# Carrying the first attention states on TensorE in a linear-attention and MLP kernel

## The chip, the cores and the metric

The kernel runs on one core of a Trainium2 chip. A core has five engines, each with its own instruction queue that it works off in order: TensorE (PE, matrix products into PSUM; its weight loads are listed apart as PEld), VectorE (DVE), ScalarE (ACT), GpSimd (POOL) and SyncE (SP), which here only issues DMAs. Engines wait for each other through semaphores. The metric is the device time of one execution in microseconds (us).

## The reference

The first half is a causal linear attention with a decay `lam` per head; its output, four batches of 768 tokens by 8 heads of 64, is read as 3072 tokens by 512 and goes through an MLP with a leaky ReLU. All is float32 in value; the two MLP weights come as float64.

```python
for b in range(nb):                      # blocks of 64 tokens
    intra = np.einsum('bhic,bhjc->bhij', qb, kb) * Dmask[None]
    intra = np.einsum('bhij,bhjd->bhid', intra, vb)
    inter = np.einsum('bhid,bhde->bhie', qb * lam_pow[None], kv_state)
    out[:, :, sl] = intra + inter
    kb_dec = kb * rev_pow[None]
    kv_state = lam_block[None, :, None, None] * kv_state + np.einsum('bhsd,bhse->bhde', kb_dec, vb)
...
h = x @ w_in                             # 3072 x 512 by 512 x 2048
g = np.maximum(0.01 * h, h)
return (g @ w_out).astype(np.float32)    # 2048 x 512
```

## The kernel before

**Attention.** The tokens are worked in 24 chunks of 128, that is two blocks of 64 per chunk, six chunks per batch. For a chunk `c`, `load_kq` and `load_v` bring keys, queries and values (two buffers each, by `c % 2`); `transposes` turns keys and queries on PE (L425), copies them from PSUM on ACT (L436, L437), scales the keys by the decay (L441, written for DVE or GpSimd) and the queries by its powers (L445: on DVE for the first QS chunks, on GpSimd after). `scores` makes on PE, in quarter-array products (helper `quad`, L335), the scores (`go`) and the two state products of the chunk (`kv`, into `pu[0]` and `pu[1]`); both lie in the PSUM tile psc, the scores in the lower and the state products in the upper half of each of its two banks. DVE multiplies the scores by the decay mask (L474) and adds the state products into one of four state tiles (L479 for the first of a batch, L481 for the others); GpSimd scales each state by the decay of a block into the next state tile (L484). `outputs` makes the chunk's result on PE: `own` (scores by values), then `inter` (state by queries) in two halves with a small copy between them (L513). The result is split at once into three parts for products in a reduced format: xh on ACT (L529), xl and xm on DVE (L530, L532).

**MLP.** Four chunks are a token group (512 tokens, six groups). The columns of the first weight are taken in eight panels `p` of 256. `w_in` loads a panel as float64 in two halves (L589, three raw buffers), turns it to float32 (ACT L610, L612, L614; DVE L616, L617) and splits it into three parts (L623 or L625, L628, L643). A unit `up(g, p)` multiplies group `g` with panel `p`: for each of two blocks of 128 columns twelve PE products (L723) into one of three PSUM banks, a rescaling on ACT (L742) between its second and third part, and the leaky ReLU on ACT (L747). Results are stored to DRAM (L754, or sums of them, L791) and read back for the second product, which runs in units of its own (`strassen`, `plain`, `ending`; L851 on PE, with loads by L825 and splits by L828, L831, L835), in parts by a Strassen scheme. Finished banks are transposed on DVE (L943) and stored (L951).

**What sets the order.** Nothing is issued directly: `add` records each step with an engine (or a choice of two), an estimated duration and the keys of the buffers that it reads and writes. `Plan.emit` orders all of them by a list scheduler: it starts each step at the earliest time that the estimates allow, and where several could start, the one of the lower rank. The rank is the position in the list `seq`, corrected by a step's own rank. `seq` is written out by hand for its first part: `('a', c)` is a whole chunk, `('b', 4)` loads and prepares chunks 4 and 5 and makes the scores of 4, `('r', c)` is a round that finishes chunk `c`, prepares `c + 2` and makes the scores of `c + 1`, `('wi', p)` prepares a panel, `('up', g, p, ...)` is a unit. Later units follow `ORDER`. The prices LEAD0 and LEAD advance the loads of the second product's units in rank, WSR delays the sums of the second weight (`w_sums`), and TURN_B sets where the rotation over the three PSUM banks starts. Where the plan expects PE to be idle for over 0.4 us, it inserts transposes of an identity matrix into an unused bank (`busy`, L282); nine more stand at the start.

## Time and profile before

| | us |
|---|---|
| median of three timed runs | 599.52 |
| lowest, highest | 599.29, 600.74 |
| the profiled execution | 598.83 |
| its span, first to last instruction | 597.1 |
| PE busy in the span | 586.2 |
| DVE, ACT, POOL busy in the span | 406.7, 299.2, 134.0 |

The granted TensorE clock is at full speed in all slices of the span. A busy share over the whole span is a mean over stages with different limits: in the first 60 us attention and the first units are worked together, from then on PE products follow each other almost without a gap, and the last 4.5 us are the drain of the output. In the lists, L and a number is a line of the kernel before; "a <- b" after a line is what was waited for; an entry with x and a number stands for that many instructions.

### The profile page before, as it was taken

What the parts mean: (1) busy time and instruction counts of PE and PEld (TensorE: products, weight loads), DVE (VectorE), ACT (ScalarE), POOL (GpSimd) and SP (SyncE); (2) the same over time, 40 slices, a digit from 0 to 9 for tenths busy, and PEclk for the clock granted to TensorE, in tenths of its full rate; (3) what the DMA queues carried; (4) which work ended last, traced back from release to release, by engine and by line L of the source; (5) the groups of instructions that cost most, each with busy time, mean ns of one, the idle gap of its engine ahead of it and who ended that gap; (6) DMA issues with size and microseconds to landing.
All of it is one profiled execution on the core that took longest, in us unless ns stands there. A gap on an engine that the chain in (4) does not pass through costs nothing.

```text
span 597.1 us, 13281 instructions
## 1 busy us (share of the span) xinstructions
PE 586.2 (98%) x5336; PEld 485.0 (81%) x5336; DVE 406.7 (68%) x559; ACT 299.2 (50%) x468; POOL 134.0 (22%) x170
## 2 busy tenths in 40 slices
PE   7899999999999999999999999999999999999997
PEld 6778888888888888888788888888888888888886
DVE  4999883357365565465389889965689695788652
ACT  3788884345555565565598874331344223252300
POOL 2654770835636348121000000000000000000000
PEclk9999999999999999999999999999999999999999
DMA  8999855975899999886788865526467547394533
GB/s 205 238 292 242 245 171 132 247 195 132 240 284 260 239 269 232 247 259 224 244 273 273 298 196 206 162 89 190 128 198 223 175 144 193 121 259 164 177 107 70
DMA packets 163949, 123.04 MB, mean 206 GB/s; under 512 B 100400, under 2 KB 140592, under 8 KB 163888
## 3 DMA queue, kind: packets, MB, share of 16 engines
q1 hardware_dynamic: 148128, 112.75, 64.4%
q10 hardware_dynamic: 13200, 5.77, 3.8%
q0 software_dynamic: 2560, 3.68, 2.5%
q8 instruction: 42, 0.69, 0.5%
q14 instruction: 19, 0.16, 0.1%
HBM read 81.27 MB, written 40.89 MB: 205 GB/s over the span
## 4 chain that ended last, share of the span: by engine, by line
PE 91%; DVE 5%; DMA 2%; ACT 0%; issue 0%; SPq 0%; DVEq 0%
PE b L723 43%; PE po L851 13%; PE b L851 12%; PE psc L851 11%; PE pt L851 4%; PE po L335 4%; PE psc L335 3%; DMA xm<-g 1%; DVE wl L628 1%; DVE w L617 1%; DMA attb<-in_q_dram 1%; DVE w L616 1%; PE pt L425 1%; DVE att L474 0%; DVE xl L530 0%
## 5 line engine op out<-in xcount | busy, mean ns | idle before, releaser
L723 PE MATMUL b<-xh,wh 128*128 128x512 f32 (+2 forms) x392 | 103.6, 387 | 0.8 <-ACT xh L529 0.8
L723 PE MATMUL b<-xm,wm 128*128 128x512 f32 (+2 forms) x392 | 103.7, 393 | 0.0
L723 PE MATMUL b<-xl,wl 128*128 128x512 f32 (+2 forms) x392 | 103.5, 386 | 0.1
L828 ACT ACTIVATE xh<-xm 128x1024 fp32r<-128x1024 f32 x46 | 48.8, 1060 | 86.6 <-DMA xm<-g 40.9
L723 PEld LDWEIGHTS b<-xh,wh 128*128 128x128 f32 x392 | 72.7, 188 | 16.1 <-ACT xh L529 0.9
L723 PEld LDWEIGHTS b<-xl,wl 128*128 128x128 f32 x392 | 72.8, 188 | 15.2 <-DVE wl L628 0.5
L723 PEld LDWEIGHTS b<-xm,wm 128*128 128x128 f32 x392 | 71.2, 188 | 15.1 <-ACT b L742 0.4
L742 ACT ACTIVATE b<-b 128x512 f32<-128x512 f32 (+2 forms) x97 | 56.1, 581 | 54.5 <-PE b L723 54.4
L747 ACT ACTIVATE gs<-b 128x512 f32<-128x512 f32 (+2 forms) x97 | 56.8, 591 | 39.7 <-PE b L723 34.6
L831 DVE SCALAR_TENSOR_TENSOR xl<-xm,xh 128x1024 fp32r<-128x1024 f32 x46 | 56.0, 1218 | 26.4 <-ACT xh L828 25.5
L835 DVE SCALAR_TENSOR_TENSOR xm<-xl,xh 128x1024 fp32r<-128x1024 f32 x50 | 61.2, 1224 | 3.5
L484 POOL TENSOR_TENSOR att<-att 128x256 f32<-128x256 f32 x40 | 34.9, 873 | 37.9 <-DVE att L481 37.9
L616 DVE TENSOR_SCALAR w<-w 128x512 int32<-128x512 int32 x32 | 22.6, 706 | 27.2 <-ACT w L610 27.1
L396 POOL DMA_DIRECT2D attb<-in_q_dram x64 | 39.5, 624 | 2.9 <-issue 1.4
L445 POOL TENSOR_TENSOR att<-att 128x512 f32<-128x512 f32 (+1 forms) x20 | 24.9, 1244 | 63.4 <-PE po L335 47.4
L441 POOL TENSOR_TENSOR attb<-attb,att 128x512 f32<-128x512 f32 (+1 forms) x23 | 26.1, 1136 | 34.6 <-PE po L425 10.5
L851 PE MATMUL psc<-xm,wm 128*128 128x512 f32 x84 | 32.8, 391 | 0.1
L851 PE MATMUL psc<-xh,wh 128*128 128x512 f32 x84 | 32.7, 389 | 0.0
L851 PE MATMUL psc<-xl,wl 128*128 128x512 f32 x84 | 32.7, 389 | 0.0
L474 DVE TENSOR_TENSOR att<-psc,att 128x512 f32<-128x512 f32 x24 | 16.5, 688 | 21.9 <-PE psc L335 21.8
L617 DVE CUSTOM_DVE_ANT_0 w<-w,lows 128x1024 uint16<-128x1024 uint16 x32 | 26.2, 818 | 7.1 <-ACT lows L614 6.2
L828 ACT ACTIVATE raws<-raws 128x1024 fp32r<-128x1024 f32 x12 | 12.7, 1061 | 27.6 <-DMA raws<-g 18.1
(184 smaller groups left out, 1096.3 us busy)
## 6 DMA issues: line engine op xcount, KB each, us to landing
xm<-b SPq DMA_DIRECT2D x28, 512.0 KB, 3.8
g<-gs SPq DMA_DIRECT2D x27, 512.0 KB, 4.6
xm<-g SPq DMA_DIRECT2D x22, 512.0 KB, 4.2
b<-gs SPq DMA_DIRECT2D x20, 512.0 KB, 3.9
raws<-in_moe_w_in_dram SPq DMA_DIRECT2D x16, 512.0 KB, 5.2
raws<-in_moe_w_out_dram SPq DMA_DIRECT2D x16, 512.0 KB, 4.9
attb<-in_k_dram SPq DMA_DIRECT2D x48, 128.0 KB, 4.7
attb<-in_v_dram SPq DMA_DIRECT2D x24, 256.0 KB, 4.7
```

The source lines that it names most:

```text
L335: nc.tensor.matmul(dst[HALF[cols]], lhsT=lhsT[HALF[rows]], rhs=rhs[HALF[rows]], start=start, stop=True, skip_group_check=True)
L396: (move if nm == "k" else carry)(0.55 if nm == "k" else QSL, lambda o=o, z=z, e=nc.sync if nm == "k" else nc.gpsimd: e.dma_start(out=o.rea ...
L484: add("POOL", 0.7, lambda new=new, j=j: nc.gpsimd.tensor_tensor(state[(j + 1) % 4], new, _bc(lam_c, 2, D), op=ALU.mult), [f"st{j % 4}", "f ...
L616: add("DVE", 0.42, lambda: nc.vector.tensor_scalar(d, d, 3, None, op0=ALU.logical_shift_left), [], [key])
L617: add("DVE", 1.0, lambda: nc.vector.tensor_tensor(d, d, low, op=ALU.add), [kl], [key])
L723: nc.tensor.matmul(dst, lhsT=w[z][:, kk * 2 * P + f * P:kk * 2 * P + (f + 1) * P], rhs=x[z][:, kk, toks], start=start and kk == 0, stop=kk ...
L742: add("ACT", ns, lambda b=b: nc.scalar.activation(out=b, in_=b, func=AF.Copy, bias=0.0, scale=S + 1.0), [], [kb], rank=-1.5)
L747: add("ACT", t, lambda o=o, x=s_: nc.scalar.activation(out=o, in_=x, func=AF.Prelu, bias=0.0, scale=(1.0 + 1.0 / S) / (WS * U), alpha=0.01 ...
L828: nc.scalar.activation(out=ring[j][0], in_=g(), func=AF.Copy, bias=0.0, scale=NEAR)
L831: nc.vector.scalar_tensor_tensor(ring[j][1], g(), 1.0, ring[j][0].bitcast(F32), op0=ALU.mult, op1=ALU.subtract)
L835: nc.vector.scalar_tensor_tensor(m, l.bitcast(F32), -S, h.bitcast(F32), op0=ALU.mult, op1=ALU.add)
L851: nc.tensor.matmul(dst, lhsT=lhs(z), rhs=ring[j][z][:, col:col + n], start=first and z == 0, stop=z == 2, skip_group_check=True)
```

## The change

The scores and the two state products get keys of their own in the plan (psc, pu0, pu1, and "began", which keeps PE's order in the shared banks). For the first two chunks (PEC = 2) the state is no longer scaled by GpSimd and added by DVE: PE multiplies the previous state by a diagonal matrix `carry_on`, which holds the block decay of each head and is built once on DVE (`factors_c`), and adds it to the state product in PSUM; ACT copies the sum to the state tile. From the last state of chunk 1 on, GpSimd and DVE carry it as before. QS goes from 4 to 2, so that the queries of chunks 2 and 3 are scaled by GpSimd; KM goes from 2 to 4, so that the keys of chunks 2 and 3 may be scaled by DVE or GpSimd, as the plan finds. TURN_B, WSR and LEAD0 are set anew. The first part of `seq`, `ORDER` and the order of some units of the first Strassen part are new. The plan gets an entry without an instruction that takes 0.45 us of the DMA queue's planned time for each output store that ACT issues.

```diff
-    QS = 4
-    KM = 2
+    QS = 2
+    KM = 4
+    PEC = 2
-    TURN_B = 2
-    HOLD, WPR, WSR, LEAD0 = 0.15, 2.0, 0.0, 12.0
+    TURN_B = 1
+    HOLD, WPR, WSR, LEAD0 = 0.15, 2.0, 2.0, 8.0
...
+    def factors_c():
+        nc.vector.tensor_tensor(carry_on, _bc(ident, 1, HP), _bc(lam_c, 2, P), op=ALU.mult)
...
+    carry_on = gst[:, 1, 0, :].rearrange("p (y t) -> p y t", y=HP)
+    add("DVE", 0.7, factors_c, ["fq"], ["gs1"])
...
         if c < GOFIRST:
-            add("PE", 0.47, go, [f"kT{i}", f"qT{i}"], ["psc"])
-        add("PE", 0.47, kv, [f"k{i}", f"v{i}"], ["psc"])
+            add("PE", 0.47, go, [f"kT{i}", f"qT{i}"], ["psc", "began"])
+        def carried(t):
+            for y in range(HP):
+                nc.tensor.matmul(pu[t][:, y, :], lhsT=carry_on[:, y, :], rhs=state[(2 * c + t - 1) % 4][:, y, :], start=False, stop=True,
+                                 skip_group_check=True)
+
+        add("PE", 0.47, kv, [f"k{i}", f"v{i}"], ["pu0", "pu1", "began"])
+        if 0 < c < PEC:
+            add("PE", 0.4, lambda: carried(0), ["gs1", f"st{(2 * c - 1) % 4}"], ["pu0", "began"])
...
-                if n == 0 and t == 0:
-                    add("DVE", 0.42, lambda new=new: nc.vector.tensor_copy(new, pu[0]), ["psc"], [f"st{j % 4}"])
+                if c < PEC:
+                    if t:
+                        add("PE", 0.4, lambda: carried(1), ["gs1", f"st{(j - 1) % 4}"], ["pu1", "began"])
+                    add("ACT", 0.42, lambda new=new, t=t: nc.scalar.copy(new, pu[t]), [f"pu{t}"], [f"st{j % 4}"])
+                elif n == 0 and t == 0:
+                    add("DVE", 0.42, lambda new=new: nc.vector.tensor_copy(new, pu[0]), ["pu0"], [f"st{j % 4}"])
                 else:
                     add("DVE", 0.42, lambda new=new, t=t: nc.vector.tensor_tensor(new, new, pu[t], op=ALU.add),
-                        ["psc"], [f"st{j % 4}"])
-                if n_pu == 2:
+                        [f"pu{t}"], [f"st{j % 4}"])
+                if n_pu == 2 and j >= 2 * PEC - 1:
                     add("POOL", 0.7, lambda new=new, j=j: nc.gpsimd.tensor_tensor(state[(j + 1) % 4], new, _bc(lam_c, 2, D), op=ALU.mult),
...
-    seq = [('a', 0), ('a', 1), ('a', 2), ('a', 3), ('wi', 5), ('b', 4), ('up', 0, 5), ('wi', 2), ('wi', 6), ('r', 4), ('r', 5), ('up', 0, 2), ('wi', 3), ('r', 6), ('up', 0, 6), ('r', 7), ('up', 0, 3), ...]
+    seq = [('a', 0), ('a', 1), ('a', 2), ('a', 3), ('b', 4), ('wi', 5), ('wi', 6), ('wi', 2), ('up', 0, 5), ('up', 0, 6), ('r', 4), ('r', 5), ('wi', 3), ('r', 6), ('up', 0, 2), ('up', 0, 3), ('up', 1, 5, 0, 3), ('wi', 4), ...]
-    ORDER = [4, 0, 3, 7, 2, 6, 5, 1]
+    ORDER = [6, 0, 2, 5, 3, 7, 4, 1]
...
-            put(("up", NG - 1, 2), ("ws", 0))
-            put(("up", NG - 1, 2), ("ws", 1))
+            put(("up", NG - 1, 1), ("ws", 0))
+            put(("up", NG - 1, 3), ("ws", 1))
...
-            seq += [s(6, 0), ("copy", "Y", "Z"), s(5, 0), ("add", "Y", "V"), s(7, 0), ("add", "V", "Z"), s(3, 0), n(2, 0), s(2, 0), n(3, 1), s(4, 0), n(2, 1), ("ws", 2), n(3, 0), ("ws", 3)]
+            seq += [s(6, 0), ("copy", "Y", "Z"), s(5, 0), ("add", "Y", "V"), s(7, 0), ("add", "V", "Z"), s(2, 0), n(3, 0), n(3, 1), n(2, 0), n(2, 1), s(4, 0), ("ws", 2), ("ws", 3), s(3, 0)]
```

## The prediction

> **What bounds the kernel now.** I began with the page's busy times and the list of what TensorE (PE) waited for.
>
> ```profile
> span 597.1 us, 13281 instructions
> PE 586.2 (98%) x5336; PEld 485.0 (81%) x5336; DVE 406.7 (68%) x559; ACT 299.2 (50%) x468; POOL 134.0 (22%) x170
> ...
> PE psc L335 <- DVE att L481: 1.8, 2, 1.1
> PE b L282 <- POOL att L285: 1.4, 1, 1.4
> PE b L723 <- ACT xh L529: 0.8, 1, 0.8
> ```
>
> PE is idle for only 597.1 - 586.2 = 10.9 us, so the first thing to find is where. A table by stretches (columns: length, then busy time of PE, weight loads, DVE, ACT and POOL with counts, clock, DMA share, GB/s) shows it.
>
> ```profile
> 0.00:15.00 15.00, 11.97 (x197) 9.35 (x201) 6.89 (x25) 5.72 (x10) 3.00 (x10) 1.00 0.84 206
> 15.00:30.00 15.00, 13.15 (x392) 10.78 (x382) 14.80 (x22) 10.61 (x20) 10.05 (x10) 1.00 0.95 238
> 30.00:45.00 15.00, 13.97 (x229) 11.12 (x229) 14.04 (x20) 12.43 (x21) 8.28 (x7) 1.00 1.05 291
> 45.00:60.00 15.00, 14.92 (x199) 12.20 (x201) 14.66 (x20) 13.07 (x24) 6.72 (x6) 1.00 0.93 241
> ...
> 300.00:360.00 60.00, 59.88 (x264) 49.01 (x264) 52.18 (x67) 51.64 (x79) 0.00 (x0) 1.00 0.81 265
> ...
> 540.00:597.10 57.10, 52.63 (x243) 43.81 (x242) 31.59 (x32) 8.65 (x9) 0.00 (x0) 1.00 0.41 120
> ```
>
> Idle PE lies in the first 60 us (3.03 + 1.85 + 1.03 + 0.08 = 6.0) and after the last product (57.1 - 52.6 = 4.5, the drain of the output, which no edit touches); 0.4 is left for 60 to 540 us. To the 6.0 come the filler transposes of line 282, which keep PE occupied but compute nothing: 30 of them, 7.3 us, all before 25.5. The first real transpose starts at 3.92, held by the first load. So 13.3 - 3.9 = 9.4 us is all that can be won at the front, and the front is the only place where anything can be won. Who sets it? DVE is 14.80 of 15 busy there. The chain that ended last, cut to the front (start, length, what), says the same.
>
> ```profile
> 8.46 0.83 PE b L282 x3
> 9.29 0.86 PE psc L335 x32
> 10.18 0.70 DVE att L474
> 10.93 0.93 PE po L335 x40
> ...
> 13.10 0.69 DVE att L445
> 13.79 0.34 DVE att L481
> 14.26 1.16 PE psc L335 x64
> ...
> 16.66 0.69 DVE att L445
> 17.36 1.14 DVE w L616
> 18.50 0.33 DVE att L481
> ...
> 22.33 0.60 DVE att L445
> ```
>
> From 16.66 to 31.04 it is DVE without a gap: states of the attention, queries, token splits, and the first weight (5). The first FFN unit starts at 28.32, when token split xh of chunk 3 exists, and gets its second third at 31.5.
>
> **The change, part by part.** The sum is against the profiled execution, 598.83 us (span 597.1 and 1.7 around it); the median of the three timed runs, 599.52, lies 0.7 above, and the forecast is stated against that median.
>
> *Keys split and state on TensorE.* Scores (psc) and state products (pu0, pu1) get keys of their own. The mask product of chunk 0 (L474) need no longer wait for the state product: scores end at 8.46, DVE is free at 7.73, so L474 ends near 9.2, under the fillers and the state product, and `own` follows that product at 10.2 instead of 10.93: 0.75 us. Scores of chunk 1 waited, by the shared key, for the state addition L481, itself queued on DVE behind L445: with the key gone they need only the query copy, which ends at 13.07, and start some 1.15 us sooner than 14.26 (these hold the 0.34 of L481; L445 of chunk 1 stays, but beside PE). DVE loses four state operations (L479 and three L481, 0.41 each); on its gapless chain only the one at 18.50 counts again, 0.33. GpSimd loses three L484 of 0.62 (states 1 to 3; the fourth stays).
>
> *Queries of chunks 2 and 3 to GpSimd.* The two L445 on the chain go: 0.69 + 0.60 = 1.29. Sum of what leaves: 0.75 + 1.15 + 0.33 + 1.29 = 3.5 us. Cross-check by occupancy: DVE works without a gap from 13.10 to 31.76, and of this 3 x 0.41 + 0.69 + 0.68 = 2.6 goes; with the 0.75 ahead of it, 3.35. The two agree.
>
> *What is added.* (a) Three groups of four PE products, 128x64 each. No row has that form; nearest from below are the four 128x128 transposes of L425, 0.42 to 0.44 us a group on the chain, from above the 32 quarter-size products, 0.86. I take 0.44, the same count and array size. The group of state 1 falls in the gap where fillers run, one of chunk 1 is hidden in its DVE wait, one I count: -0.44 (ends 0 and -2.6). (b) Four ACT copies from PSUM, like L436's 0.58 for twice the width and L479's 0.41: ACT is 10.6 of 15 busy, so they have room, but they queue behind the weight conversions (rivals). (c) `factors_c`, one DVE product near 0.7 (L445): it comes after the power scans end at 6.58 (its tile is half of gs1, first needed by a unit after 37 us), and DVE idles from 7.73 to 10.18; zero, its cover being that idle time; without it 0.7. The keys' scaling of chunk 0 can go to GpSimd, idle until 10.79, instead. (d) KM 4 lets the keys of chunks 2 and 3 be scaled on DVE (0.66) in place of GpSimd (1.05); DVE is the later engine then, so I expect it seldom: -0.15 (ends 0 and -1.3). (e) GpSimd gets two L445 (1.28 and 1.51 in the rows of chunks 4 and 5) and loses three L484 (1.86): +0.9 us. DVE work beside GpSimd was stretched: L616 to 1.23 from 0.42, L617 to 1.19 from 0.69, L628 to 1.64 from 1.22, L643 to 1.98 from 1.22, L532 to 0.82 from 0.68: 2.6 us over 13.5 us of GpSimd work from 10 to 32, or 0.2 per us: -0.16 (ends +0.3, if the lost L484 were the ones that hurt, and -1.6, if each new operation costs the 0.8 of the worst row).
>
> The Trainium skill, page "SBUF — State Buffer", section "Who interferes with whom", has the harsher rule: a DVE instruction with two SBUF inputs and a GpSimd one that reads SBUF exclude each other, and the later blocks fully. The row agrees: L616 began at 17.27, GpSimd's L441 ran 17.16 to 18.21, and L616 ended 0.29 after it. By that rule (e) is at its lower end and the sum 1.3 (rival 2).
>
> *Order of the first units.* Chunks 4 and 5 now come ahead of weight 5, weights 6 and 2 ahead of the first unit, and unit 6 ahead of rounds 4 and 5, which used to stand before the second unit; weights 4 and 0 are due later. DVE work due before a given unit is the same for the second and less by weight 4 and round 7 for the fifth. A weight costs DVE 2 x (0.42 + 0.69) + 2 x 1.22 = 4.7 to 6 us. The DMA queue keeps its loads, in another order; raw weights find three buffers as before. PE lost 0.5 us between 31.8 and 60; I count no gain (ends +0.5 and -1.5: one weight load waited 1.6 for its transfer). TURN_B 1 makes the third product block use b11, not b2, which PE waited for by 0.1.
>
> *The later settings.* LEAD0 12 to 8, WSR 0 to 2, ORDER, the two early sums and the store entries of the plan change who comes first at 300 to 400 us. PE is 59.88 of 60 busy there, so 0.1 at most is won. I take zero; the cover is the products in between.
>
> Sum: 3.5 - 0.44 - 0.15 - 0.16 = 2.75 us. 599.52 - 2.75 = 596.8 (against the profiled run 596.1).
>
> **The rivals.**
> 1. *Front limited elsewhere.* After 31 us DVE is 14.0 to 14.7 of 15 busy and the DMA share is 0.93 to 1.05. If weights cannot come sooner, units start early and starve. For: these shares. Against: a single DMA wait of 1.6 us, and DVE's removed work is gone for good. It keeps the 0.5 to 1.0 of the key split: 598.8.
> 2. *GpSimd takes back what DVE was spared.* Both query operations block a DVE operation like L616's (0.8 each): 2.75 - 1.45 = 1.3, or 598.2. The Trainium skill's rule above says that it is so where the operation beside them has two SBUF inputs. For: the five stretched rows; against: mask products, state additions and xl read PSUM and kept their 0.68 and 0.41.
> 3. *More.* Chain and new order add up: unit 1 starts 3.5 sooner, fillers between go too, the 0.5 after 31 is recovered: 4.5 in all, 595.0.
> 4. *Slower, by the ACT queue.* A state copy behind three weight conversions (0.67 + 0.78 + 0.77 = 2.2) holds the carried product, and PE's queue, with the next scores, behind it. Three such waits take 6.6 - 2.75: 603.4; two waits, 601.2. It decides from 4.6 us of waits. Against: only one copy in four need fall so, as other PE work is planned between.
> 5. *Slower, at 341 to 358 us.* The SP queue held two stores from 341.15 to 348.95 before the next unit's load (349.11), whose transfer, ACT and two DVE steps end at 358.23, just as PE starts on it at 358.27. No slack: with less lead, a load behind one more store (a unit is 24 x 0.227 = 5.4 us of PE) stalls PE by 5.4: 599.52 - 2.75 + 5.4 = 602.2. It decides from 4.6 us. Against: the same change reorders the units there, and four of them need no new weight sums.
>
> **How the numbers follow.** A difference below 0.3% (1.8 us) is about what a measurement of this kernel cannot tell from no change; faster means below 597.7. Forecast 0.50 (own range 595.7 to 598.0; 0.42 of it faster, 0.08 same), rival 1 0.10 and rival 2 0.07 (same), rival 3 0.13 (faster), rival 4 0.08 and rival 5 0.12 (slower). So faster 0.55, same 0.25, slower 0.20. The range from 595.0 to 601.0 leaves out most of rivals 4 and 5 below their milder forms, and the far end of 3.
>
> **What would show it.** Right: L474 of chunk 0 near 8.5; scores of chunk 1 near 12.5; no DVE L445 after chunk 1; first xh,wh product near 25.5 and filler time below 6; PE idle after 30 below 0.7. Wrong: PE waits on ACT state copies above 1 us each; L616 to L643 stretched by more than 4 us in sum before 32; weight splits ending later than unit 2 needs; a PE wait above 1 us between 300 and 400 us. The prediction fails most easily by the plan itself, since every queue's order is written anew by a list scheduler whose costs shift with each edit.

## The result and the profile after

| | before | after |
|---|---|---|
| median, us | 599.35 (8 runs) | 602.65 (8 runs) |
| lowest, highest, us | 598.01, 600.74 | 601.46, 604.26 |
| the profiled execution, us | 598.83 | 604.26 |
| its span, us | 597.1 | 602.5 |

The ratio is 1.0059, 95% interval 1.0043 to 1.0076: the change makes the kernel 0.59% slower. Forecast were 596.8 us and a gain; the time lies outside the range and on the other side. The lines of the changed kernel have other numbers: L335 is now L342 (quarter-array products), L425 L432 (transposes), L445 L452 (queries scaled), L474 L488 (mask product), L481 L499, L484 L502, L529 and L530 L547 and L548, L616 and L617 L634 and L635, L628 L646, L643 L661, L723 L741. L610, a weight conversion on ACT, is now L628, a number that stood for a weight split before. New is L478, the carried product.

The busy times of the changed kernel:

```profile
span 602.5 us, 13353 instructions
PE 591.7 (98%) x5361; PEld 489.8 (81%) x5361; DVE 404.0 (67%) x556; ACT 300.7 (50%) x471; POOL 133.4 (22%) x168
```

The span grew by 5.4 us, PE's busy time by 591.7 - 586.2 = 5.5, its idle time not at all. So in this execution PE does not wait longer, it is occupied longer. The table by stretches (columns as in the prediction) says where.

```profile
0.00:15.00 15.00, 13.20 (x231) 11.21 (x231) 7.63 (x25) 6.01 (x10) 1.80 (x8) 1.00 0.85 203
15.00:30.00 15.00, 12.91 (x362) 9.96 (x360) 12.41 (x20) 10.08 (x19) 9.62 (x8) 1.00 0.99 249
30.00:45.00 15.00, 14.46 (x152) 11.75 (x156) 13.21 (x18) 11.43 (x21) 8.86 (x7) 0.89 0.82 221
45.00:60.00 15.00, 13.64 (x265) 11.23 (x257) 14.62 (x20) 10.95 (x21) 5.91 (x5) 0.94 0.89 252
300.00:360.00 60.00, 59.74 (x263) 48.39 (x262) 49.26 (x65) 51.28 (x80) 0.00 (x0) 1.00 0.76 251
```

Three things are to be seen. DVE was in fact unloaded: 12.41 us busy from 15 to 30, where it had 14.80. The granted clock fell to 0.89 and 0.94 of full speed in two rows after the front, (0.11 + 0.06) x 15 = 2.6 us of clock; the second stretch at half clock runs on past 60 us, and in all 3.4 us are lost. And from 300 to 360 us PE is busy for 59.74, before 59.88: nothing happened late.

From 60 to 540 us PE is idle for 0.4 us before and for 0.5 after. So a gain had to show in the first 60 us, as less idle time or less filler time of PE. Idle it is there for 1.80 + 2.09 + 0.54 + 1.36 = 5.8 us, before 6.0; the fillers take 6.95 us (31 of them), before 7.35. That is 0.6 us less, where some 3.5 were forecast. The carried products, 3.3 us in this stretch, and the lost clock come on top.

The chain that ended last, cut to the front (start, length, what):

```profile
7.01 1.16 PE psc L342 x64
...
9.82 1.04 PE psc L478 x8
...
12.50 1.16 PE psc L342 x64
13.66 1.05 PE psc L478 x8
14.71 0.02 issue
14.73 0.70 DVE att L488
15.43 0.04 issue
15.48 0.69 PE po L342 x32
16.17 1.03 PE psc L478 x8
...
27.09 2.23 DVE wl L646
29.32 0.02 issue
29.34 0.17 ACT w L628
29.51 0.40 issue
29.92 0.58 ACT xh L547
30.50 0.04 issue
30.54 3.60 PE b L741 x8
```

The scores of chunk 1 start at 12.50, where the forecast had them (before 14.26). But all three groups of carried products stand in the chain, at 1.04, 1.05 and 1.03 us, and by the scores of chunk 2, at 18.86, the lead is gone (before 18.88). Then the weight split of panel 5 takes 2.23 us, a weight conversion on ACT waits for it, xh of chunk 3 stands behind that conversion in ACT's queue, and the first unit starts at 30.54 in place of 28.32. Its first eight products take 3.60 us, before 2.10.

VectorE's own list, the operations of this stretch that waited (the bracket is the idle time ahead and what ended it), and the weight split:

```profile
14.73 0.69 DVE L488 TENSOR_TENSOR att<-psc,att 128x512 f32<-128x512 f32 x1 [0.97 <-PE psc L478]
...
17.67 0.16 DVE L531 COPY att<-po 128x2 f32<-128x2 f32 x1 [1.31 <-PE po L342]
...
20.83 0.69 DVE L488 TENSOR_TENSOR att<-psc,att 128x512 f32<-128x512 f32 x1 [0.77 <-PE psc L342]
...
27.01 2.30 DVE L646 SCALAR_TENSOR_TENSOR wl<-wh,w 128x1024 fp32r<-128x1024 f32 x1
29.82 0.42 DVE L499 TENSOR_TENSOR att<-att,psc 128x256 f32<-128x256 f32 x1 [0.51 <-POOL att L502]
```

Before, DVE had no gap above 0.2 us from 13.1 to 31.8. Now it waits 0.97 + 1.31 + 0.77 + 0.51 = 3.6 us, three of the four times for PE: the work taken from DVE came back as waiting.

Two explanations were in hand, which do not exclude each other. One: the carried products, a little over 1 us a group on the path, take back what the front won. The other: GpSimd, busy with attention beside DVE's first weight split, stretches it (2.30 us; the same split takes 1.22 in its undisturbed rows) and so delays the first unit. Rivals to both: the new order or the later settings cost it, or the waits named are only the last of several.

### The profile page after: what moved, and what is told of

It is laid out like the page before. It is cut to its first block, busy times and chain, and to the rows that moved or that the text cites. A ratio compares the mean times of both kernels' runs of the same rounds, so it can differ in the third digit from the quotient of the medians.

```text
span 602.5 us, 13353 instructions
## 1 busy us (share of the span) xinstructions
PE 591.7 (98%) x5361; PEld 489.8 (81%) x5361; DVE 404.0 (67%) x556; ACT 300.7 (50%) x471; POOL 133.4 (22%) x168
## 4 chain that ended last, share of the span: by engine, by line
PE 95%; DVE 2%; ACT 1%; DMA 1%; issue 0%; ACTq 0%; DVEq 0%
PE b L741 44%; PE po L869 13%; PE b L869 13%; PE psc L869 11%; PE pt L869 4%; PE po L342 4%; PE psc L342 4%; PE pt L432 1%; DVE w L635 1%; DMA attb<-in_k_dram 1%; PE psc L478 1%; PE b L432 0%; DVE att L488 0%; PE po L432 0%; DVE wl L646 0%
## 5 line engine op out<-in xcount | busy, mean ns | idle before, releaser
L741 PE MATMUL b<-xh,wh 128*128 128x512 f32 (+2 forms) x392 | 105.9, 394 | 1.1 <-ACT xh L547 1.1
L741 PE MATMUL b<-xm,wm 128*128 128x512 f32 (+2 forms) x392 | 105.0, 395 | 0.8 <-issue 0.8
L741 PE MATMUL b<-xl,wl 128*128 128x512 f32 (+2 forms) x392 | 103.2, 386 | 0.0
L741 PEld LDWEIGHTS b<-xh,wh 128*128 128x128 f32 x392 | 74.2, 192 | 17.0 <-ACT xh L547 1.3
L741 PEld LDWEIGHTS b<-xl,wl 128*128 128x128 f32 x392 | 73.2, 188 | 14.8
L741 PEld LDWEIGHTS b<-xm,wm 128*128 128x128 f32 x392 | 71.2, 189 | 16.9 <-ACT b L760 1.2
L502 POOL TENSOR_TENSOR att<-att 128x256 f32<-128x256 f32 x37 | 29.8, 804 | 75.9 <-DVE att L499 65.0
L452 POOL TENSOR_TENSOR att<-att 128x512 f32<-128x512 f32 (+1 forms) x22 | 30.4, 1381 | 33.0 <-DVE w L634 9.8
L635 DVE CUSTOM_DVE_ANT_0 w<-w,lows 128x1024 uint16<-128x1024 uint16 x32 | 29.3, 916 | 10.3 <-ACT lows L632 9.1
L499 DVE TENSOR_TENSOR att<-att,psc 128x256 f32<-128x256 f32 x37 | 15.3, 414 | 30.7 <-PE psc L342 28.3
L869 PE MATMUL psc<-xh,wh 128*128 128x512 f32 x80 | 31.1, 389 | 0.0
L869 PE MATMUL psc<-xl,wl 128*128 128x512 f32 x80 | 31.1, 389 | 0.0
L869 PE MATMUL psc<-xm,wm 128*128 128x512 f32 x80 | 31.1, 389 | 0.0
L869 PE MATMUL b<-xm,wm 128*128 128x512 f32 x74 | 28.8, 389 | 0.0
L869 PE MATMUL b<-xh,wh 128*128 128x512 f32 x74 | 28.8, 389 | 0.0
```

The costliest lines, as they stand in the source:

```text
L452: add(eng, us, lambda: e.tensor_tensor(o, x, _bc(pow_q, 2, 2)[:, :, m, :], op=ALU.mult), ["fq", dep], [f"qsT{i}"])
L502: add("POOL", 0.7, lambda new=new, j=j: nc.gpsimd.tensor_tensor(state[(j + 1) % 4], new, _bc(lam_c, 2, D), op=ALU.mult), [f"st{j % 4}", "f ...
L635: add("DVE", 1.0, lambda: nc.vector.tensor_tensor(d, d, low, op=ALU.add), [kl], [key])
L741: nc.tensor.matmul(dst, lhsT=w[z][:, kk * 2 * P + f * P:kk * 2 * P + (f + 1) * P], rhs=x[z][:, kk, toks], start=start and kk == 0, stop=kk ...
L869: nc.tensor.matmul(dst, lhsT=lhs(z), rhs=ring[j][z][:, col:col + n], start=first and z == 0, stop=z == 2, skip_group_check=True)
```

## The experiments

Each kernel was timed in turn with the kernel before on one chip; its ratio is to that. A ratio of 0.001 is 0.6 us. The changed kernel, run again as it is:

> The changed kernel once more, unaltered, to see which of its stalls recur. Its recorded execution had two stretches of half TensorE clock (about 31 to 34.7 and 58.5 to 61.5 us, together 3.4 us of lost clock) and a gap of 0.77 us in the middle of a product near 57 us. Theory A (the added PE work sets the loss; the half-clock stretches are an accident of one execution): median 602 to 603 again, and a profile that is at full clock or nearly so and has a span near 600.5 to 601. Rival B (the half clock follows from this order of work and makes the loss): every execution shows at least one such stretch of 1.5 us or more of lost clock, in the same place.

Measured: 602.44 us, ratio 1.0050 (1.0032 to 1.0068). The slowdown repeats, some 3.0 to 3.5 us. Its profiled span is 600.9 us, with one half-clock stretch before the end in place of two. By the mean granted clock of each timed run, (1 - clock) x span, the clock cost 1.1 us a run here and 0.6 in the 23 runs of the kernel before beside it: about half a microsecond of the three.

**The carried products.** They were cut to one of four in each group, then doubled, which leaves every queue's order as it is.

```diff
         def carried(t):
-            for y in range(HP):
+            for y in range(1):                          # e1
+            for y in [*range(HP), *range(HP)]:          # e10
```

> The changed kernel with only the first of the four products in each carried group; the states of three of four head pairs in the first batch are left uncarried between the first blocks, so that part of the computation is missing. Every queue's order, every wait and all other work are as in the changed kernel. A carried group takes 1.04 us on the chain there, three times; one product of four should take 0.27. Theory A (these products lie on the chain, PE being busy from 4 to 20 us): 3 x 0.77 = 2.3 us less than the changed kernel, about 600.3. Rival C (the front is set by DVE, ACT and GpSimd, and PE only fills the time): at most 0.5 us less, 602.2 or more.

> The changed kernel with each carried group made twice (eight products; the first batch's carried states come out twice too large); order of all queues unchanged. Theory A (a carried group is fully on the path): 3 x 1.05 = 3.1 us more than the changed kernel, 605.4 to 605.8. Rival C (part of it is hidden): 1.5 us more or less, at most 604.1.

Measured: 600.78 us, ratio 1.0019 (0.9999 to 1.0039), and 604.52 us, 1.0083 (1.0063 to 1.0104). The second group in PE's list, first with one of four, then as it is in the changed kernel, then doubled:

```profile
13.02 0.43 PE L478 MATMUL psc<-att,gs 128*128 128x64 f32 x2
```

```profile
13.59 1.10 PE L478 MATMUL psc<-att,gs 128*128 128x64 f32 x8
```

```profile
14.78 2.00 PE L478 MATMUL psc<-att,gs 128*128 128x64 f32 x16
```

The records of the three groups together go from 1.3 to 3.3 to 6.0 us, and the time by +1.9 (1.0050 against 1.0019) and +2.0 us (1.0083 against 1.0050), each with an uncertainty of 1.6. From one of four to doubled it is 3.8 us, uncertain by 1.7, for 4.7 us of records, some 0.8 us of time for each us of carried products: they lie on the path, with little slack. One product is two records at 1.10 / 8 = 0.14 us each, with weight loads of 0.19 us that partly overlap. Halving the number of elements against a transpose (128x64 for 128x128) bought nothing; the four transposes of L425, 0.60 to 0.66 us in the front, have one record each where four carried products have eight.

**No carried products, and queries back on DVE.** One part of the change undone at a time; both rewrite the plan.

```diff
-    PEC = 2                                             # e2
+    PEC = 0
```

```diff
-    QS = 2                                              # e3
-    KM = 4
+    QS = 4
+    KM = 2
```

> The changed kernel with PEC = 0 and without building the diagonal matrix: states are carried by GpSimd and DVE as before, all else (queries of chunks 2 and 3 on GpSimd, new order, later settings) stays. Theory A: without 3.1 us of PE work on the chain, but with four state operations back on DVE (0.41 each, of which some 0.7 to 1.1 on its chain), 600.3 to 601. Rival D (the carry is harmless and the new order of units and weights, with the queries on GpSimd, makes the loss): 602 to 603.5, the first unit's first product still after 30 us.

> The changed kernel with QS = 4 and KM = 2: queries of chunks 2 and 3 back on DVE, keys of these chunks on GpSimd alone. Theory A: these two matter little, 602 to 603.5. Rival E (GpSimd beside DVE makes the loss: the weight split took 2.30 us in place of 1.22 beside two GpSimd operations and held ACT's queue and the first unit): 600.5 to 601.5, the split below 1.7 us and the first unit's first product before 29 us.

Measured: 601.05 us, ratio 1.0031 (1.0015 to 1.0046), and 605.46 us, 1.0101 (1.0081 to 1.0121). Without any carrying 1.1 us comes back (uncertain by 1.4), not the three, though the state operations that return to DVE and the new plan stand in this number too. With the queries of chunks 2 and 3 on DVE, in the new order, the kernel is 3.1 us slower still, of which 1.4 is clock (2.5 us lost a run, against 1.1). The split of panel 5 takes its 1.22 us there. So no sign is left that the moved queries are the harm in this order. PE waited 2.0 us for a weight part on DVE there (wh, L643 of that kernel).

One carried group alone, with the state product of chunk 1 as before:

```diff
-    PEC = 2                                             # f3
+    PEC = 1
```

> The changed kernel with PEC = 1: only the second state of chunk 0 is carried by TensorE, one group in place of three, and chunk 1's states go over GpSimd and DVE. Computes all. The plan moves somewhat. Theory A: two groups less, 2.1 us of PE work at 0.65 to 0.75 of it on the path, against three state operations back on DVE (1.2 us): 601.3 to 602.2. Rival: the replanned order decides, anything beyond 1.5 us from the changed kernel.

Measured: 602.06 us, ratio 1.0052 (1.0032 to 1.0072), its runs spread from 600.18 to 604.64. It can't be told from the changed kernel, and the count of groups alone doesn't give the time once the plan is rewritten; the clean comparison is e1 with e10.

**Parts of the change alone.** The new keys and the plan's store entries in the kernel before (e4; "keys" below means both), with the carried products (e5), with the query settings (e6); and the changed kernel with the first order of before (e7).

```diff
-            add("PE", 0.47, go, [f"kT{i}", f"qT{i}"], ["psc"])
-        add("PE", 0.47, kv, [f"k{i}", f"v{i}"], ["psc"])
+            add("PE", 0.47, go, [f"kT{i}", f"qT{i}"], ["psc", "began"])
+        add("PE", 0.47, kv, [f"k{i}", f"v{i}"], ["pu0", "pu1", "began"])
...
+    PEC = 0                                             # e4, e6; 2 in e5
...
-    QS = 4                                              # e6 alone
-    KM = 2
+    QS = 2
+    KM = 4
```

```diff
-    seq = [('a', 0), ('a', 1), ('a', 2), ('a', 3), ('b', 4), ('wi', 5), ('wi', 6), ('wi', 2), ('up', 0, 5), ('up', 0, 6), ...]
+    seq = [('a', 0), ('a', 1), ('a', 2), ('a', 3), ('wi', 5), ('b', 4), ('up', 0, 5), ('wi', 2), ('wi', 6), ('r', 4), ...]   # e7
```

> The kernel before with the new keys of the plan alone (psc, pu0, pu1, began) and the store entries: no carried products, queries and keys as before, all orders and settings as before. No operation is added or removed, only the planned order moves. Prediction on record: the split lets the mask product of chunk 0 start near 8.5 and is worth 0.75 + 1.15 of the 3.5 us, so 597.5. Theory F (the split exists in the plan only; the first mask product still waits for all products in its PSUM tile, as in the changed kernel, where the one of chunk 1 waited for the carried group): no gain, 598.8 to 600.3, and the mask product of chunk 0 starts after the state product.

> The kernel before with the new keys and the carried products (PEC = 2); queries, keys' scaling, orders and settings as before. Theory A (a carried group takes 1.04 us on the chain): 1 to 2 us above the kernel with the keys alone, about 601. Rival G (the carry is worth its removed DVE operations when the order is the old one, and only costs in the new order): equal to or below the kernel with the keys alone.

> The kernel before with the new keys and QS = 2, KM = 4; no carry, orders and settings as before. Prediction on record: two DVE operations leave a gapless DVE chain, 1.0 to 1.3 us below the kernel with the keys alone. Rival E (GpSimd takes it back by stretching DVE): equal or up to 1 us above it.

> The changed kernel with the first part of the order list as before (weight 5 ahead of chunks 4 and 5, unit 2 after rounds 4 and 5); carry, queries, keys, ORDER and later settings as in the changed kernel. Theory A with the new first order as the second cause (the changed kernel without the carry was still 1.7 us above the kernel before): 1 to 2 us below the changed kernel, 600.5 to 601.5, and the first unit's first product before 29.5 us. Rival H (the first order is harmless, what is left comes from the later settings): 602 to 603, and PE idle by over 1 us between 240 and 400 us.

| | us | ratio | 95% interval |
|---|---|---|---|
| e4, keys alone | 611.78 | 1.0210 | 1.0182 to 1.0237 |
| e5, keys and carried products | 616.60 | 1.0280 | 1.0255 to 1.0306 |
| e6, keys and queries | 615.54 | 1.0261 | 1.0228 to 1.0294 |
| e7, changed, first order of before | 612.61 | 1.0221 | 1.0200 to 1.0241 |

The keys and store entries, which issue no instruction, cost 12.6 us by themselves (2.6 of it clock), for the list scheduler then writes other queues for the whole kernel, and the units starve late. Which of the two does it, no run here tells. Two rows of the kernel with the keys alone:

```profile
240.00:300.00 60.00, 56.24 (x696) 46.23 (x696) 26.38 (x54) 30.48 (x54) 12.61 (x15) 0.97 0.72 220
360.00:420.00 60.00, 57.34 (x251) 46.62 (x250) 48.23 (x53) 24.91 (x32) 0.00 (x0) 1.00 0.51 166
```

and of the changed kernel:

```profile
240.00:300.00 60.00, 59.72 (x778) 49.08 (x777) 28.55 (x58) 33.27 (x59) 14.44 (x18) 1.00 0.81 247
360.00:420.00 60.00, 60.00 (x266) 49.72 (x265) 47.36 (x53) 21.14 (x26) 0.00 (x0) 1.00 0.53 165
```

With the keys alone PE is idle for 3.8 and 2.7 us of these rows, in the changed kernel for 0.3 and 0. The new first order is worth 10 us to the changed kernel (e7 against c0), most of it late: from 240 to 420 us PE is idle for 6.4 us in e7 and for 0.5 in the changed kernel, while the first unit starts at 30.62 and 30.54. So the order is no addition to the change: it repairs what the keys do to the plan, and no part can be priced alone against the kernel before. The later settings were undone alone in no run. In e4 the mask product of chunk 0, whose key no longer names the state products, still starts only after them, having waited 1.3 us for PE (L489 is the mask product there; the state product ended at 8.73, the scores at 7.62):

```profile
8.80 0.69 DVE L489 TENSOR_TENSOR att<-psc,att 128x512 f32<-128x512 f32 x1 [1.30 <-PE psc L343]
```

Removing a key of the plan did not remove the wait; both lie in one PSUM tile. The carried group ahead of L488 at 14.73 in the list above is the same case: with one of four products, all, and twice as many, the mask product of chunk 1 starts 0.04 us after the group's end (13.49, 14.73, 16.82). The Trainium skill, page "PSUM — Partial Sum Buffer", section "PSUM bank collisions raise a hardware error ⚠️", has the rule that would have said so: PSUM is to be guarded by bank and quadrant, not by address. The trace agrees in that the reader of one half of a bank waited 0.97 us for a write to the other half; whether the bank or the tile is what the wait was set for, no run here tells.

**The wait on ACT ahead of the first unit.** The conversion for which xh stands in the queue waits because panel 6 goes into a tile that the split of panel 5 still reads. Here panel 6 gets another tile; alone (e8) and with one carried product of four (e9).

```diff
+        dst = gst[:, 1] if p == 6 else w32
         for h in range(2):
-            to_float32("wi", p, h, w32[:, h, :], f"w32{h}")
-        parts(p, w32f, ["w320", "w321"])
+            to_float32("wi", p, h, dst[:, h, :], f"w32{h}")
+        parts(p, dst.rearrange("p h n -> p (h n)"), ["w320", "w321"])
```

> The changed kernel with the float32 form of the second panel (6) in the free half of the tile gs in place of the shared w tile; every queue keeps its order. In three executions of the changed kernel's front ACT's first conversion of that panel waited 1.43 to 1.50 us for the split wl of panel 5, which took 2.30 in place of 1.22 us, and the token split xh of chunk 3 stood behind it, and the first unit behind that (30.54 and 30.79 us, against 28.32 in the kernel before). Theory J (this queueing is the second cause): ACT's wait gone, first product near 29.2, 1.0 to 1.5 us below the changed kernel, 601.0 to 601.5. Rival K (the units are then held by the next late input): first product earlier, time within 0.4 us of the changed kernel.

> Both at once: the own buffer for panel 6 and one of four products in each carried group (three of four head pairs of the first batch are left uncarried between the first blocks). One of four alone gave 600.8 against 602.4 to 602.7. Theory A + J (two separate costs): 599.3 to 600.0, equal to the kernel before within its spread; first product near 27.7 us. Rival K: 600.5 to 601, as with one of four alone.

Measured: 602.70 us, ratio 1.0051 (1.0029 to 1.0073), and 600.79 us, 1.0022 (1.0007 to 1.0037): the same as without the buffer in both cases. Taken together the two comparisons give 0.1 us slower, uncertain by 1.1. In e8 the first product does start earlier, at 29.08 in place of 30.54, but PE then waits 0.8 us, until 32.02, for the token split xl of chunk 3. That stands behind both weight splits of panel 5 in DVE's queue (L646, still 2.30 us, and L661) and starts at 31.29, in the changed kernel at 31.30. Later PE waits 0.3 and 0.9 us for parts of panel 6, at 38.38 and 40.44. The ACT wait was in the chain and was worth nothing that can be measured; behind the first product stood DVE's queue.

**GpSimd beside the weight split.** GpSimd's list in the changed kernel at the time of the split (27.01 to 29.31):

```profile
26.60 1.62 POOL L452 TENSOR_TENSOR att<-att 128x512 f32<-128x512 f32 x1 [1.16 <-ACT att L444]
28.19 1.60 POOL L502 TENSOR_TENSOR att<-att 128x256 f32<-128x256 f32 x1
```

The first are the queries of chunk 4, which GpSimd scaled before the change too. In e11 it scales only a quarter of them; in f4 DVE scales them; in f2 the queries that the change moved, those of chunks 2 and 3, are shortened instead (to half of those of chunk 2 and a quarter of those of chunk 3).

```diff
+            ys = slice(0, 1) if c == 4 else slice(0, HP)                       # e11; c == 3, and m cut for c == 2, in f2
-            add(eng, us, lambda: e.tensor_tensor(o, x, _bc(pow_q, 2, 2)[:, :, m, :], op=ALU.mult), ["fq", dep], [f"qsT{i}"])
+            add(eng, us, lambda: e.tensor_tensor(o[:, ys], x[:, ys], _bc(pow_q, 2, 2)[:, ys, m, :], op=ALU.mult), ["fq", dep], [f"qsT{i}"])
...
-            o, x = (z.rearrange("p y (t i) -> p y t i", t=2)[:, :, m, :] for z in (qsTs[i], pt if c < QS else qTs[i]))
+            o, x = (z.rearrange("p y (t i) -> p y t i", t=2)[:, :, m, :] for z in (qsTs[i], pt if c < QS or c == 4 else qTs[i]))   # f4
```

> The changed kernel with GpSimd scaling only a quarter of the queries of chunk 4 (the rest of that chunk's queries stay as they are, so that part is missing). This operation (1.62 us) runs beside the split wl of panel 5. Order unchanged. Theory J (GpSimd beside DVE stretches the split, which holds ACT and the first unit): the split falls from 2.30 to 1.8 us or less, first product 0.5 us or more earlier, 0.4 to 1.0 us below the changed kernel. Rival L (the split's length comes from something else): split unchanged at 2.3, no difference.

> The changed kernel with the queries of chunk 4 scaled by DVE (0.69 us from PSUM) in place of GpSimd (1.62 beside the split). Computes all. Theory E: DVE pays 0.69 and gets back 0.8 of the split and GpSimd's later operations start sooner: 0.3 to 1.2 us below the changed kernel. Rival: equal or slower, as when the queries of chunks 2 and 3 were put back on DVE (605.5).

> The changed kernel with GpSimd scaling half of the queries of chunk 2 and a quarter of those of chunk 3 (the rest of these chunks' queries keep old values, so that part is missing); order unchanged. If the moved query operations cost time where they run now (DVE stretched beside them: 0.39 for the weight step at 17.8 us, 0.28 for the token split at 21.8): 0.5 to 1.0 us below the changed kernel. If they lie in DVE's waits: within 0.3 us of it.

| | us | ratio | 95% interval |
|---|---|---|---|
| e11, a quarter of chunk 4's | 601.09 | 1.0022 | 1.0008 to 1.0037 |
| f4, chunk 4's on DVE | 601.45 | 1.0030 | 1.0014 to 1.0046 |
| f2, less of those of chunks 2 and 3 | 602.74 | 1.0057 | 1.0037 to 1.0078 |

The split in e11, from DVE's list:

```profile
26.90 1.48 DVE L647 SCALAR_TENSOR_TENSOR wl<-wh,w 128x1024 fp32r<-128x1024 f32 x1
```

It takes 1.48 us in place of 2.30, and 1.21 in f4; the time falls by about 1.7 us in e11 (uncertain by 1.4), and by 1.2 in f4 (also by 1.4, so not clear of noise), where the plan is new and DVE has 0.68 us of queries more. Less of the moved operations gives nothing. The cost is GpSimd's, but of an operation that the change didn't touch: what it moved is when this operation and the split meet. Before the change the two splits of panel 5 met GpSimd operations too:

```profile
26.05 1.07 POOL L484 TENSOR_TENSOR att<-att 128x256 f32<-128x256 f32 x1
26.57 1.64 DVE L628 SCALAR_TENSOR_TENSOR wl<-wh,w 128x1024 fp32r<-128x1024 f32 x1
27.84 1.51 POOL L445 TENSOR_TENSOR att<-att 128x512 f32<-128x512 f32 x1 [0.72 <-ACT att L437]
28.46 1.98 DVE L643 SCALAR_TENSOR_TENSOR wm<-wl,wh 128x1024 fp32r<-128x1024 f32 x1
```

In all four cases (these two, the changed kernel and e11) the split ends 1.08 to 1.09 us after the end of the GpSimd operation that had begun ahead of it: it got little done until then. In f4, where the split began ahead (28.39 against 28.54), it took 1.21 us and the GpSimd operation 1.55. The Trainium skill, page "SBUF — State Buffer", section "Who interferes with whom", states that a DVE instruction with two SBUF inputs contends with a GpSimd instruction that reads SBUF. The trace agrees: the split reads two SBUF tiles, and it ran for 2.30 us beside GpSimd operations that read SBUF.

The stretch is no newcomer: before, the two splits were longer by 0.42 + 0.76 = 1.2 us than alone, after by 1.1 and 0. e11 says what the operation costs the changed kernel, not what the change made it cost; the kernel before was not run with it shortened.

**Both causes together, and the query load.** One carried product of four and a quarter of chunk 4's queries (f1, the edits of e1 and e11):

> One of four products in each carried group and a quarter of GpSimd's query scaling of chunk 4 (both left out in part, as in the two runs before); order of all queues as in the changed kernel. Theory A + E (two separate costs, 1.7 and 1.4 us): 599.2 to 599.8, equal to the kernel before. Rival M (both open the same later wait): 600.6 or more, no better than the better of the two.

Measured: 600.25 us, ratio 1.0020 (1.0002 to 1.0037), the same as either alone. The gains do not add up, and PE's list of f1 shows the next wait, at the transposes of chunk 5's queries:

```profile
28.02 0.44 PE L432 MATMUL pt<-att,attb 128*128 128x128 f32 x2 [1.06 <-DMA attb<-in_q_dram]
29.18 0.69 PE L432 MATMUL pt<-att,attb 128*128 128x128 f32 x2 [0.73 <-DMA attb<-in_q_dram]
29.52 3.29 PE L742 MATMUL b<-xh,wh 128*128 128x512 f32 x8
```

PE waits 1.8 us for chunk 5's queries there (2.6 with earlier query loads), 2.0 in e1 and 2.4 in e9; in the changed kernel it was 0.3 in one profile and 1.0 in the other, and before it did not show. SP issued the load of chunk 5's queries at 23.20 in the changed kernel and at 21.08 before, since it now stands behind the keys and values of chunk 4 and ran behind the keys alone. It is the plan with carried products that turns this order, not the new order of the units: with the first order of before the values are still ahead (e7, 22.40 and 22.88), and so they are in the kernel before with keys and carried products (e5, 22.04 and 22.55); with one carried group (f3) or none (e2, e4, e6) the queries are ahead (in e4 at 20.75, the values at 21.85). The last two kernels issue it ahead of chunk 4's keys: the changed kernel with this one edit (g1), and f1 with it (g2).

```diff
             def go(y=y, dst=dst, nm=nm):
+                pairs = [] if c == 5 and nm == "q" else [(y, dst)]
+                if c == 4 and nm == "k":
+                    pairs = [q5[0], (y, dst)]
-                for z in range(2):
-                    nc.sync.dma_start(out=dst[:, z * HP:(z + 1) * HP, :], in_=y[z::2].rearrange("h p d -> p h d"))
+                for yy, dd in pairs:
+                    for z in range(2):
+                        nc.sync.dma_start(out=dd[:, z * HP:(z + 1) * HP, :], in_=yy[z::2].rearrange("h p d -> p h d"))
```

> The changed kernel, complete, with one thing moved: SyncE issues the query load of chunk 5 ahead of the key load of chunk 4 rather than after the key and value loads of chunk 4. Theory N (what stops the gains of the carried products and of the shortened queries from adding up is that TensorE then waits for this load): in the changed kernel itself the wait was only 0.3 us in one profile and 1.0 in another, so 0.3 to 0.6 us below the changed kernel, some 602.0 us. Rival R (the key and value loads of chunk 4, now behind it, come late in its stead): equal or slower, 602.5 to 603.5 us, with TensorE or GpSimd waiting for in_k_dram or in_v_dram of chunk 4.

> One carried product of four in each carried group, a quarter of chunk 4's queries scaled, and the query load of chunk 5 issued ahead of the key load of chunk 4. Leaves out: three quarters of the state carried within chunks 0 and 1, and three quarters of the scaling of chunk 4's queries. Theory N: the 2.3 to 2.9 us in which TensorE waited for the query load in the kernel with both shortened are what kept the two gains from adding up; without it the first unit's first product comes before 29 us and the time is 599.0 to 599.5 us, about 1 us below the 600.3 of that kernel. Rival R: the wait turns into one for the key or value load of chunk 4, or into one that is none of the loads; 600.0 to 600.8 us.

Measured: g1 602.70 us, ratio 1.0044 (1.0028 to 1.0060), g2 599.71 us, 1.0000 (0.9988 to 1.0013). PE's list of g2 at the same place:

```profile
26.73 0.66 PE L441 MATMUL pt<-att,attb 128*128 128x128 f32 x4
28.16 2.12 PE L751 MATMUL b<-xh,wh 128*128 128x512 f32 x8 [0.77 <-ACT xh L557]
```

No wait for a query load is left, the first unit starts at 28.16 at full clock, and the kernel is as fast as before the change. Against f1 that is 1.2 us with an uncertainty of 1.3, so the step is carried by the wait that went (2.6 us for query loads to none) more than by the timing; 0.8 of it is clock that was not lost (1.1 us a run in f1, 0.3 in g2). For g1 the gain of 0.4 us against c0 is below what the runs can tell, as is right for a wait of 0.3 to 1.0 us.

So three things hold the time of the changed kernel: the size of the carried products, GpSimd's operation beside the weight split, and the later query load. Each takes over where another is removed, and with all three cut back the slowdown is gone within the measurement. They are not three shares of it: the GpSimd operation stood there before the change, and the query load came to stand late by the carried products. What the change added to PE's path is the 3.1 us of these products, and of what it took from DVE 0.6 us show on PE. No kernel tried was faster than the one before, and g2, which equals it, leaves work out.

## Why the prediction was wrong

Starts of the front's main steps in the traces, us:

| | before | after | g2 |
|---|---|---|---|
| mask product of chunk 0 | 10.18 | 8.27 | 8.66 |
| scores of chunk 1 | 14.26 | 12.50 | 12.24 |
| mask product of chunk 1 | 15.48 | 14.73 | 13.80 |
| scores of chunk 2 | 18.88 | 18.86 | 17.26 |
| mask product of chunk 2 | 20.12 | 20.83 | 19.26 |
| mask product of chunk 3 | 24.90 | 25.48 | 23.91 |
| first product of the first unit | 28.32 | 30.54 | 28.16 |

- *What bounds the kernel.* Right: the 3.3 us are won or lost around the first 60 us, nothing later moves.
- *Keys split, 0.75 and 1.15.* Both times came (8.27 for a forecast 8.5, 12.50 for 12.5), the first by luck: the state product now ran straight behind the scores, without fillers between, and ended at 8.18, before DVE was free at 8.27, so there was nothing to wait for; in e4 there was, and the mask product waited 1.30 us. The plan's keys are not DVE's waits, and the mask product of chunk 1, free of the state product by its key, waited 0.97 us for the carried group in the same tile. The scores of chunk 1 did lose their wait for the state addition, here and in e4 (11.73). But pricing the keys as one edit was idle: with the store entries they cost 12.6 us alone.
- *(a) Carried products, -0.44.* This step failed first. Measured were 1.05 us a group, three on the path: 3.1, more than the lower end of 2.6. The row chosen, transposes of the same array size, was the nearer one by shape and the wrong one by kind: it has one record for a product where the carried product has two, each with its weight load. Its price was low as well: the transposes on the front's chain took 0.60 (at 11.86 and 15.43), and the 0.44 is from 33.60 us on. Of the two covers named, the fillers hid nothing for chunk 0 (9.75 lies behind `own`, not among the fillers), and the DVE wait of chunk 1 became DVE waiting for PE.
- *Queries to GpSimd and 0.33 of state addition, 1.6.* The DVE time did go (14.80 to 12.41 from 15 to 30), but the cross-check by occupancy, which took DVE for the bound throughout, failed: with less to do it waited 3.6 us, mostly for PE, and PE's idle and filler time fell by 0.6 us in place of 3.5. Even g2, with carried products of 0.43 a group, keeps only 1.0 us of lead at the mask product of chunk 3, and 0.2 at the first unit.
- *(b), (c)* ACT copies and `factors_c` cost nothing seen: the carried groups start without a wait for ACT. (d) came true for chunk 2 (18.79, 0.68 us on DVE). The times of rivals 4 and 5 (601.2 to 603.4, and 602.2) came true without their mechanisms.
- *(e) and rival 2.* The mechanism was right, the operation wrong. (L616, the prediction's row for the Trainium skill's rule on two SBUF inputs, reads one tensor and a constant; the weight splits are the rows for it.) DVE work before 32 us is stretched by 2.6 us in sum, as before (L646 by 1.1, the two L635 by 0.9, L634 and L550 by 0.6), but the largest piece now falls on the first split of panel 5, behind which ACT's conversion and the token split xl wait; e11 prices it at 1.7 us when shortened alone. The operations that the change moved cost nothing (f2).
- *Order of the first units, zero.* Right for the front: with the first order of before the first unit starts at 30.62, with the new one at 30.54 (e7). Wrong for the kernel, where the order wins back 10 us of what the keys lose. "The DMA queue keeps its loads, in another order" left out what that other order does, which came with the carried products: chunk 5's query load behind the values of chunk 4, for which PE waits once it is early enough to notice. This is rival 1 in small: not weights but queries limit the front.
- *Later settings, zero, and rival 5.* Right for the changed kernel as a whole: 59.74 of 60 busy from 300 to 360 us. As a price of the edit it stays open, since no run undoes them alone.
- *The sum.* It added gains along one engine's queue as though its end alone set the next start. The lead was 1.8 us at the scores of chunk 1 and gone at those of chunk 2, two carried groups later; from there on the mask products start later than before. Behind PE's own work, GpSimd's operation beside the split and the query load stood next, as e1, e11 and f1 show.

## What to carry to other kernels

Before counting time taken from a busy engine as won, look up for each station on its path who would be second to arrive, and by how much; the gain ends there. Price a small product by its weight loads and its records per product, not by its elements, and ask on which path it stands. Where a list scheduler writes the queues, an edit has no price of its own, and a key removed from the plan did not remove the wait on a shared PSUM tile.

## What the runs showed of the hardware

The granted clock fell after stretches in which PE was only partly idle. Two pairs of neighbouring windows of the changed kernel (clock in the third column from the end); the first unit's first product begins in the first pair:

```profile
27.36:30.77 3.41, 1.95 (x26) 1.19 (x25) 2.90 (x3) 1.92 (x5) 2.88 (x3) 1.00 0.98 263
30.77:34.18 3.41, 3.41 (x10) 2.52 (x10) 3.34 (x5) 2.08 (x4) 2.33 (x2) 0.50 0.98 309
54.67:58.08 3.41, 2.05 (x41) 1.32 (x32) 3.34 (x7) 1.55 (x3) 1.63 (x1) 1.00 0.99 276
58.08:61.49 3.41, 3.41 (x10) 2.66 (x9) 2.77 (x5) 2.17 (x4) 1.89 (x2) 0.50 0.41 94
```

Both half-clock stretches last 3.41 us, and the second begins seven such lengths after the first ended (58.08 - 34.18 = 23.9). So the windows to look at seem to be those of a grid of 3.41 us, which is how these four are cut. Ahead of the drops PE was busy for 1.95 and 2.05 of 3.41 us, with no gap above 1.1 us. But a window of e2 on its grid, 38.79 to 42.20 us, with PE busy for 1.86, left the clock at 1.00, so the share of the records alone doesn't decide it. The Trainium skill, page "TensorE: Matmul & The Clock Gate", section "What's actually happening", says that the gate looks at a free-running window and drops after an idle one; the free-running part agrees with the grid, while "idle" was here no more than 43% idle. Ahead of the second drop PE waited 0.59 us for DVE and 0.77 us in the middle of a product at 56.9, for which the trace names no releaser; this stretch did not appear in c0, and the cause of that gap stays open.
